# The first product of the first expert, first batch: from float32r halves to float16 pairs

## The chip, the core and the metric

The kernel runs on one core of a Trainium2 chip. The metric is the device time of one execution in microseconds, the median of several runs. A core has a matrix engine (TensorE, PE in the profile, with its weight loads as PEld), a vector engine (VectorE, DVE), an activation engine (ScalarE, ACT), GpSimd (POOL), and a queue engine (SyncE, SP) that issues the transfers. Every engine works through its own queue in the order in which the program was written, and waits by semaphores for the others.

## The reference

Attention over 2 batches, 8 heads, 576 positions and 64 channels, with rotary positions; its output, 1152 tokens of 512 numbers, goes through two experts in a row:

```python
def _moe_ref(x, w_a, w_b, w_out):      # 512 -> 1536 -> 512
    a = x @ w_a
    b = x @ w_b
    return (a * b @ w_out).astype(np.float32)

def _moe2_ref(x, w_in, w_out):         # 512 -> 2048 -> 512
    h = x @ w_in
    sp = np.where(h > 20.0, h, np.log1p(np.exp(np.minimum(h, 20.0))))
    g = h * np.tanh(sp)
    return (g @ w_out).astype(np.float32)
```

Inputs and output are float32. The weights arrive as float64 words (`in_w_dram`), and three VectorE instructions turn a block of 128 x 512 of them into float32 (`xw<-wr`).

## The kernel before

A number is kept as a high and a low part, and a product of two such numbers as three matrix products (high with high, high with low, low with high: `PASSES`). The parts are either both float16 after scaling by a power of two, or float32r, a rounded float32 that the matrix engine takes in one pass.

A recording layer (`Plan`) collects every operation with a priority (`at(t)`), a planned cost and its dependences, and then writes out one fixed order for every engine (`Plan.order`). `any_` operations go to VectorE or GpSimd, as the planner sees fit. So constants such as `W_LEAD`, `U0`, `U1` or `G` change no arithmetic; they change priorities, and by them the order.

The stages in order of time, with "unit" for one block of 128 query rows of a head (72 units in all):

- Attention of batch 0 (units 0 to 35, `attend0`), whose end overlaps the next.
- Attention of batch 1 (units 36 to 71, `attend`): scores `s`, row maximum `m` on VectorE, exponential on ScalarE, split `pp` into float16 pairs, a transposing DMA `pt`, product with the values `o`, and a transpose `xt` into `x`, again split into two parts. Woven into it, as matrix work that is always ready, lie layer 1 of the first expert for batch 0 (`layer1(0)`: for each of 12 steps f the tiles of w_a and of w_b, k = 0 and 1, each for 256 and for 320 tokens, 12 matrix instructions per tile) and then layer 2 (`layer2(0)`).
- Layer 1 and layer 2 for batch 1 (`layer1(1)`, `layer2(1)`), with 27 blocks of the second expert's weights converted ahead (`store_ahead`).
- The second expert, in two token groups (`hidden_two`, `accumulate`).

In `layer1(0)` a weight block is converted, copied to float32r high (ACT `w<-xw`), its remainder taken by `any_`, kept in DRAM as float32 (`ka<-xw`), and its absolute sum taken on ScalarE (`junk`, into `w_sum`). After layer 1 one matrix instruction adds `w_sum` over the partitions (`w1s`), and `power` turns the sums into powers of two, up and down (`w_up`, `w_dn`). `layer1(1)` loads the float32 blocks back (`wc<-ka`) and splits them with these scales into float16 pairs (ACT and DVE `w<-wc,w_up`); there the tokens of batch 1 are float16 pairs too. So batch 0 multiplies float32r and batch 1 float16, in the same shapes.

Of the kernel before, what the change touches and what calls it, by code (L numbers as in the profile page):

```python
# [38 lines left out]
FSLACK = 1300  # L39
FBIAS = 200  # L40
MARGIN = 0
D1 = 6
D4 = 2
# [357 lines left out]
W_LEAD = 7  # L401
PE_LAG = 0
LOAD_LEAD = 12
OFF = dict(S=-7, M=-8, E=-8, P=0.5, T=-0.5, V=4, N=-2, X=-4)
R0, R1 = 0.233, 0.73
U0, U1 = 1.766, 3.358
C0 = 8
F0 = 2
T_L1 = 3
Y_LATE = 30  # L410
Q_REST = 7
T_B = 12
LOAD_A = 16
HOLD = 40
# [10 lines left out]
YS = 12  # L425
S0_AT = 20
W3S = 28
# [4 lines left out]
O_LEAD = 2  # L432
FA = 1
# [12 lines left out]
VP = (8, 5, 8)  # L446
V_AT = 5
V_BOUND = 23
# [13 lines left out]
G = 1.495  # L462
# [17 lines left out]
def lo32(ap):  # L480
    return ap.bitcast(F32)
# [3 lines left out]
def kernel(ctx: ExitStack, tc: tile.TileContext, qk, v5, w1, w2, w34, tab, out):  # L485
# [43 lines left out]
    rings = dict(raw=(w_p, 3), xw=(w_p, 3))  # L529
# [13 lines left out]
    n_o = len(AHEAD) - NF2  # L543
# [7 lines left out]
    l1_dn = w_p.tile([128, 2 * NF1], F32, tag="l1_dn", name="l1_dn")  # L551
# [16 lines left out]
    def weights(  # L568
# [42 lines left out]
        if not split:  # L611
            return None
# [93 lines left out]
    x_dn = w_p.tile([128, 1], F32, tag="x_dn", name="x_dn")  # L706
# [222 lines left out]
    def transpose_x(p, part):  # L929

        early = p == SPLIT
        if not part:
            if p < NP:
                xT[p] = x_p.tile([128, 2, S], F32R, tag=f"x{p}", name=f"x{p}")
            else:
                xT[p] = x_p.tile([128, 2, 2 * S + 128], F16, tag=f"x{p}", name=f"x{p}")[:, :, 0:S]
# [18 lines left out]
        for t, c, n in parts:  # L955
            if p // NP in PLAIN1:
                act.copy(lo32(x[:, 0, c]), t[:, 0:n])
                continue
# [11 lines left out]
    def l1_tile(b, f, k, hf, w, t1):  # L970
# [3 lines left out]
        t = l_ps.tile([128, 512], F32, tag="l", name=f"l1_{b}_{f}_{hf}_{k}")  # L974
        i = 0
        for c in range(NM):
            x = xT[b * NP + c]
            if b in PLAIN1:
                pe.matmul(t[:, :n], lhsT=lo32(w[:, 0, c, :]), rhs=lo32(x[:, 0, sl]), start=(c == 0), stop=(c == NM - 1))
                continue  # L980
            for ws, xs in PASSES:
                pe.matmul(t[:, :n], lhsT=w[:, ws, c, :], rhs=x[:, xs, sl], start=(i == 0), stop=(i == 11))
                i += 1
        at(t1 - W_LEAD)
        if k == 0:
            ap, bufs = (rc_p, ASB) if b else (w_p, AS0)
            a_sb[hf] = ap.tile([128, S - TA], F32, tag="a_sb", name="a_sb", bufs=bufs)[:, :n]
            if b:
                act.activation(a_sb[hf], t[:, :n], AF.Copy, scale=l1_dn[:, 2 * f : 2 * f + 1])
            else:  # L990
                act.copy(a_sb[hf], t[:, :n])
        else:
# [7 lines left out]
            if b:  # L1000
                q = t[:, :n]
                dve.scalar_tensor_tensor(q, q, l1_dn[:, 2 * f + 1 : 2 * f + 2], p, op0=ALU.mult, op1=ALU.mult)
            else:
                q = p
                dve.tensor_tensor(q, p, t[:, :n], op=ALU.mult)
            act.copy(ab[:, 0, :], q)
            AB_ENG = dve if b else any_
            AB_ENG.tensor_tensor(ab[:, 1, :], q, lo32(ab[:, 0, :]), op=ALU.subtract)

    def layer1(b, t0, dt, early, between=None):  # L1010
# [3 lines left out]
        held = {}  # L1014
        for f, k, halves in steps:
            w = held.get((f, k))
            if w is None:
                if between:
                    between(2 * f + k, t0)
                i = 2 * f + k  # L1020
                w = weights(
                    t0 - W_LEAD,
                    w1[i],
                    hold=t0 - HOLD,
                    plain=b in PLAIN1,
                    cached=f"a{i}",
                    keep=f"a{i}" if i in KEEP1 else None,
                    stat=None if b else i,
                    half=w_up[:, i : i + 1] if b else None,
                )  # L1030
                w = held[f, k] = w.rearrange("p s (c j) -> p s c j", c=NM)
            for hf in halves:
                l1_tile(b, f, k, hf, w, t0)
                t0 += 2 * dt * (HALF[hf].stop - HALF[hf].start) / S
        return t0
# [146 lines left out]
    ab_cm = ab_p = l_cm = l_ps = None  # L1182
    plan.slack = SLACK[0]
    for n in range(NU):
# [8 lines left out]
        (attend0 if n < NU // 2 else attend)(n)  # L1193
        if n in PRE:
# [6 lines left out]
        if n == V_AT:  # L1201
# [3 lines left out]
            v_scale(1, NP)  # L1205
            v_split(1)
            v_split(2)
        if n == V_BOUND:
# [5 lines left out]
            dve.tensor_reduce(x_dn, v_mx[:, NP:], axis=AX.X, op=ALU.max)  # L1214
            dve.tensor_scalar_mul(v_x[:, NP:], v_up[:, NP:], x_dn)
# [23 lines left out]
    t = l_ps.tile([128, 512], F32, tag="l", name="w1s")  # L1239
    n1 = 2 * NF1  # L1240
    power(t[:, 0:n1], w_sum[:, 0:n1], w_up[:, 0:n1], w_dn[:, 0:n1])
    dve.tensor_scalar_mul(l1_dn, w_dn[:, 0:n1], x_dn)
# [9 lines left out]
    rings.update(raw=(rc_p, R6), xw=(rc_p, X6), rawc=(c_p, RC))  # L1252
# [167 lines left out]
    rings.update(raw=(w_p, 3), xw=(w_p, 3))  # L1420
# [142 lines left out]
```

## Time and profile before

| what | value |
|---|---|
| median of 3 runs | 562.15 us (561.83 to 562.51) |
| the profiled execution | 561.03 us, of which the span of the trace is 559.2 us |
| PE busy | 543.6 us, 97% of the span |
| PEld busy (weight loads, beside PE) | 429.3 us, 77% |
| DVE busy | 473.9 us, 85% |
| ACT busy | 356.1 us, 64% |
| POOL busy | 137.9 us, 25% |
| TensorE clock granted, mean over the span | 0.993 of full speed |

The ends of matrix instructions are modelled in the trace, and consecutive ones overlap. So the time that one costs is the distance from its start to the next start, not its duration. The bounds of the stages, read from the first and last instruction of their tiles: attention of batch 0 up to 94.2 us, attention of batch 1 with the last row maximum at 237.7, layer 1 of batch 1 from 263.5 to 337, layer 2 of batch 1 until the second expert begins at 372.

### The profile page before, as it was taken

The numbers are of one execution on the slowest core, as the hardware profiler recorded it, in microseconds if no ns is written. First come the engines' busy times: TensorE is split into PE (matmuls) and PEld (weight loads), VectorE is DVE, ScalarE is ACT, GpSimd is POOL, SyncE is SP. The second block draws the span as 40 slices with busy tenths as digits, with TensorE's granted clock in tenths as the row PEclk, the third lists the DMA queues.
The fourth block names the chain that finished last, engine by engine and source line by source line (L and its number), as shares of the span: only waits on it lengthen the run. The fifth ranks groups of instructions, "written<-read, shape, count | busy, mean of one in ns | idle before, by whom it ended". The sixth has DMA issues, their size and how long they took to land.

```text
span 559.2 us, 11791 instructions
## 1 busy us (share of the span) xinstructions
PE 543.6 (97%) x4416; PEld 429.3 (77%) x4416; DVE 473.9 (85%) x897; ACT 356.1 (64%) x731; POOL 137.9 (25%) x176
## 2 busy tenths in 40 slices
PE   7999999999999999999999999999999999999997
PEld 5778778889888988899876789997666776555553
DVE  5998999999999999977998899879999997554542
ACT  3879788677687786545676765369676545343440
POOL 1577657520221010110004002636430200000000
PEclk9899999999999999999999999999999999999999
DMA  8336556899999999999987379684779465431002
GB/s 318 108 107 208 170 163 186 229 231 210 280 234 216 256 247 252 272 235 373 386 275 273 95 248 349 237 273 147 263 270 331 170 199 193 136 100 62 1 0 94
DMA packets 92200, 117.40 MB, mean 210 GB/s; under 512 B 52080, under 2 KB 58224, under 8 KB 92144
## 3 DMA queue, kind: packets, MB, share of 16 engines
q1 hardware_dynamic: 92144, 116.66, 69.7%
q8 instruction: 34, 0.56, 0.4%
q14 instruction: 22, 0.18, 0.1%
HBM read 77.82 MB, written 27.53 MB: 188 GB/s over the span
## 4 chain that ended last, share of the span: by engine, by line
PE 77%; DVE 11%; ACT 4%; DMA 3%; issue 3%; SPq 1%; POOL 1%; DVEq 0%; ACTq 0%; POOLq 0%
PE l L397 31%; PE acc L397 16%; PE h L397 13%; PE s L397 7%; PE o L397 6%; PE tm L397 2%; DVE xw L397 2%; DVE m L397 2%; DMA wr<-in_w_dram 2%; DVE pp L397 1%; DVE w L397 1%; DMA qkr_k<-in_qk_dram 1%; DMA wc<-ka 1%; DVE wv L397 1%; SPq L397 1%
## 5 line engine op out<-in xcount | busy, mean ns | idle before, releaser
L397 PE MATMUL l<-x,w 128*128 128x320 f32 (+3 forms) x1152 | 157.8, 294 | 0.0
L397 PE MATMUL acc<-w,g 128*128 128x512 f16 (+1 forms) x432 | 103.4, 383 | 0.0
L397 DVE SCALAR_TENSOR_TENSOR xw<-wr,xw 128x512 uint32<-128x512 uint32 x136 | 96.9, 718 | 1.0
L397 PEld LDWEIGHTS <-wv 128*128 128x128 f16 x672 | 64.9, 98 | 27.7 <-issue 5.2
L397 PE MATMUL l<-ab,w 128*128 128x320 f32 (+1 forms) x576 | 81.3, 299 | 0.1
L397 PEld LDWEIGHTS l<-x,w 128*128 128x128 f32 x576 | 78.2, 190 | 3.0 <-issue 2.7
L397 PEld LDWEIGHTS l<-ab,w 128*128 128x128 f32 x576 | 77.5, 190 | 1.2 <-issue 0.8
L397 PEld LDWEIGHTS <-w 128*128 128x128 f16 x576 | 56.1, 98 | 14.4 <-issue 0.2
L397 PEld LDWEIGHTS <-g 128*128 128x128 f16 x372 | 36.3, 98 | 36.4
L397 DVE TENSOR_TENSOR hb<-h,hb 128x256 f32<-128x256 f32 (+1 forms) x112 | 47.7, 450 | 13.5 <-PE h L397 11.5
L397 PE MATMUL h<-sp,wv 128*128 128x256 f16 (+1 forms) x384 | 57.5, 286 | 0.5 <-DVE hb L397 0.5
L397 DVE TENSOR_REDUCE m<-s 128x1 f32<-128x576 f32 x72 | 51.9, 748 | 4.4 <-PE s L397 3.6
L397 PE MATMUL s<-qk 64*128 64x288 f32 x256 | 44.4, 439 | 2.3 <-DVE qk L397 1.4
L397 ACT ACTIVATE junk<-xw 128x512 f32<-128x512 f32 x51 | 32.5, 637 | 21.9 <-DVE xw L397 21.0
L397 ACT ACTIVATE hb<-hb,two_dn 128x512 f32<-128x512 f32 (+1 forms) x32 | 24.7, 773 | 32.2 <-DVE hb L397 32.2
L397 PE MATMUL h<-y,wv 128*128 128x256 f16 (+1 forms) x288 | 43.3, 286 | 0.4 <-DVE hb L397 0.3
L397 PEld LDWEIGHTS s<-qk 64*128 64x128 f32 x256 | 25.4, 190 | 10.9 <-issue 4.8
L397 ACT ACTIVATE s<-s,m 128x576 f32<-128x576 f32 x36 | 25.3, 715 | 11.6 <-DVE m L397 11.2
L397 DVE TENSOR_SCALAR xw<-wr 128x512 uint32<-128x512 uint32 x68 | 31.4, 471 | 0.2 <-DMA wr<-in_w_dram 0.2
L397 DVE SCALAR_TENSOR_TENSOR g<-hb,g_up,g 128x640 f16<-128x640 f32 (+1 forms) x27 | 24.1, 894 | 6.4 <-ACT g L397 5.7
L397 DVE SCALAR_TENSOR_TENSOR w<-wc,o_up,w 128x512 f16<-128x512 f32 x16 | 11.9, 750 | 20.3 <-ACT w L397 20.2
L397 POOL TENSOR_TENSOR w<-xw,w 128x512 fp32r<-128x512 f32 x10 | 13.7, 1365 | 62.3 <-ACT w L397 59.2
(186 smaller groups left out, 936.7 us busy)
## 6 DMA issues: line engine op xcount, KB each, us to landing
wr<-in_w_dram SPq DMA_DIRECT2D x68, 512.0 KB, 5.2
kc<-xw SPq DMA_DIRECT2D x32, 256.0 KB, 4.2
qkr<-in_qk_dram SPq DMA_DIRECT2D x14, 576.0 KB, 4.5
wc<-kc SPq DMA_DIRECT2D x27, 256.0 KB, 3.7
ka<-xw SPq DMA_DIRECT2D x24, 256.0 KB, 2.7
wc<-ka SPq DMA_DIRECT2D x24, 256.0 KB, 5.2
wt<-kc SPq DMA_DIRECT2D x16, 256.0 KB, 3.7
kwt<-wv SPq DMA_DIRECT2D x8, 512.0 KB, 3.8
```

The lines of the kernel that those rows point to most:

```text
L397: getattr(engine, method)(*map(real, args), **{k: real(v) for k, v in kw.items()})
```

## The change

Layer 1 of batch 0 multiplies float16 pairs too. For this the weights' scale has to be known before their step, not after the layer: `layer1(0)` loads the blocks of step f + 1 during step f (`load_w1`), adds their `w_sum` over the partitions with a matrix instruction into two spare columns of the bank of step f's own tile (`sum_w1`, after k = 0 and 320 tokens), makes the powers of two with four small VectorE instructions (`scale_w1`), and splits (`split_w1`). The tokens of batch 0 are scaled on their way out of `xt`. The pairs, not the float32 blocks, are kept in DRAM, and `layer1(1)` loads them straight into the weight tiles, with no split. The product of both scales now sits in the copy of the a-half (`ab_dn`), so the multiplication with the b-half has no scale any more. One block fewer is converted ahead (`AHEAD`: 26), so that one more step of the second expert's output product for the first token group runs in float32r. The order's constants are changed as well.

```diff
-U0, U1 = 1.766, 3.358
+U0, U1 = 1.654, 3.432
-F0 = 2
+F0 = 1
-QC = 128
+QC = 256
-AHEAD = (0, 2, 3, 5, 7, 8, 10, 12, 13, 15, 17, 18, 20, 22, 23, 25, 24, 26, 27, 28, 29, 30, 31, 32, 33, 34, 35)
+AHEAD = (0, 2, 3, 5, 7, 8, 10, 12, 14, 15, 17, 20, 22, 23, 24, 25, 26, 27, 28, 29, 30, 31, 32, 33, 34, 35)
-YS = 12
+YS = 9
-G = 1.495
+G = 1.373
...
-            act.copy(x[:, 0, c], t[:, 0:n])
-            hi = lo32(x[:, 0, c]) if p < NP else x[:, 0, c]
-            dve.tensor_tensor(x[:, 1, c], t[:, 0:n], hi, op=ALU.subtract)
+            if p < NP:
+                act.activation(hi, t[:, 0:n], AF.Copy, scale=x_up)
+                dve.scalar_tensor_tensor(lo, t[:, 0:n], x_up, hi, op0=ALU.mult, op1=ALU.subtract)
...
+        if g and SUM_LAST:
+            sum_w1(sums, g, g + 1)
...
-            if b:
-                act.activation(a_sb[hf], t[:, :n], AF.Copy, scale=l1_dn[:, 2 * f : 2 * f + 1])
-            else:
-                act.copy(a_sb[hf], t[:, :n])
+            act.activation(a_sb[hf], t[:, :n], AF.Copy, scale=ab_dn[:, b, f : f + 1])
...
+    def sum_w1(t, f0, f1):
+        pe.matmul(t, lhsT=ones_w, rhs=w_sum[:, 2 * f0 : 2 * f1], start=True, stop=True)
+
+    def scale_w1(t, f0, f1, t0):
+        c = slice(2 * f0, 2 * f1)
+        at(t0 - W_LEAD - P_LEAD)
+        up = w_up[:, c]
+        dve.tensor_scalar(up, t, 1e-30, 1e30, op0=ALU.max, op1=ALU.min)
+        up = up.bitcast(U32)
+        dve.tensor_scalar(up, up, 0x7F800000, 0x7F800000, op0=ALU.bitwise_and, op1=ALU.bitwise_xor)
+        dve.reciprocal(w_dn[:, c], up.bitcast(F32))
+        two = w_dn[:, c].rearrange("p (f t) -> p f t", t=2)
+        dve.scalar_tensor_tensor(
+            ab_dn[:, 0, f0:f1], two[:, :, 0], x_dn2[:, 0:1], two[:, :, 1], op0=ALU.mult, op1=ALU.mult
+        )
+
+    def split_w1(f, t0, dt):
+        for i in (2 * f, 2 * f + 1):
+            at(t0 - W_LEAD + i % 2 * dt)
+            w, up, r = new(0, i), w_up[:, i : i + 1], raw0[i]
+            act.activation(w[:, 0, :], r, AF.Copy, scale=up)
...
+                dve.scalar_tensor_tensor(w[:, 1, :], r, up, w[:, 0, :], op0=ALU.mult, op1=ALU.subtract)
+            held0[i] = w
+            kept[f"a{i}"] = d_p.tile([128, 2, 512], F16, tag=f"ka{i}", name=f"ka{i}")
+            sp.dma_start(kept[f"a{i}"], w)
```

What the new order does is shown at three places. The first is VectorE in layer 1 of batch 0, at step 6 (`l_0_6_...`: batch 0, step 6, token half, k). Before, the weights' remainder `w<-xw` stands wherever VectorE has room:

```order
L397 TENSOR_TENSOR w_2633<-xw_2527,w_2633 128x512
L397 RECIPROCAL den_1_1_2664<-den_1_1_2664 128x2
L397 TENSOR_TENSOR pp_2657<-s_2553,pp_2657 128x576
L397 TENSOR_TENSOR a_sb<-a_sb,l_0_6_0_1_2631 128x256
L397 SCALAR_TENSOR_TENSOR xw_2623<-wr_2490,xw_2623 128x512
L397 TENSOR_TENSOR w_2690<-xw_2533,w_2690 128x512
L397 TENSOR_REDUCE m_2708<-s_2687 128x1
```

After, at the same step, `w_0_14` is the first weight block of step 7:

```order
L397 TENSOR_SCALAR w_up<-l_0_6_1_0_2569 128x2
L397 SCALAR_TENSOR_TENSOR vhl_113<-v_1963,v_up,vhl_113 128x10x64
L397 TENSOR_SCALAR w_up<-w_up 128x2
L397 SCALAR_TENSOR_TENSOR xw_2589<-wr_2399,xw_2589 128x512
L397 RECIPROCAL w_dn<-w_up 128x2
L397 TENSOR_TENSOR a_sb<-l_0_6_0_1_2647,a_sb 128x256
L397 SCALAR_TENSOR_TENSOR ab_dn<-w_dn,x_dn_679 128x1
L397 SCALAR_TENSOR_TENSOR w_0_14_2670<-xw_2320,w_up,w_0_14_2670 128x512
```

Between the product of step 6 and the weights of step 7 there now lie eight VectorE instructions, the first of which reads a bank that the matrix engine has just written. On the matrix engine the same place, after, with step 6's two k tiles on either side of the new sum:

```order
L397 LDWEIGHTS w_0_12_2537
L397 MATMUL l_0_6_1_0_2569<-x_1655,w_0_12_2537 128x320
L397 MATMUL l_0_6_1_0_2569<-w_sum,ones_w 128x2
L397 LDWEIGHTS w_0_13_2575
L397 MATMUL l_0_6_0_1_2647<-x_820,w_0_13_2575 128x256
```

What follows there are 24 products of step 6 and 14 products of the attention, then step 7. The sums of steps 1 to 11 stand like this; step 0 has a sum of its own in the attention of batch 0.

The third place is VectorE at the end of the attention. `x<-xt` is the split of the last token block, `y_mx` the maxima of layer 2's eight tiles. Before, three of the eight come behind it (the third, `l_0_3_1`, seven instructions below these), with splits of batch 1's weights between them:

```order
L397 TENSOR_TENSOR x_4137<-xt_3968,x_4137 128x576
L397 TENSOR_REDUCE y_mx<-l_0_2_1_4073 128x1
L397 SCALAR_TENSOR_TENSOR w_4195<-wc_4156,w_up,w_4195 128x512
L397 SCALAR_TENSOR_TENSOR w_4207<-wc_4162,w_up,w_4207 128x512
L397 SCALAR_TENSOR_TENSOR w_4221<-wc_4167,w_up,w_4221 128x512
L397 TENSOR_SCALAR xw_4246<-wr_4172 128x512
L397 TENSOR_REDUCE y_mx<-l_0_3_0_4176 128x1
```

After, one does:

```order
L397 TENSOR_TENSOR pp_4152<-s_4072,pp_4152 128x576
L397 RECIPROCAL den_0_2_4182<-den_0_2_4182 128x2
L397 TENSOR_REDUCE y_mx<-l_0_3_0_4154 128x1
L397 RECIPROCAL den_1_3_4266<-den_1_3_4266 128x2
L397 TENSOR_TENSOR x_4283<-xt_4161,x_4283 128x576
L397 TENSOR_REDUCE y_mx<-l_0_3_1_4240 128x1
```

So the end of the attention has moved back against layer 2 of batch 0: on the matrix engine 90 products of that layer follow the last transpose `xt` before the change, and 21 after it.

## Rows read from the trace of the kernel before

**Rows 1.** Three stretches: length, busy us of PE, PEld, DVE, ACT, POOL; clock, DMA, GB/s:

```profile
94.20:237.70 143.50, 142.04 (x1331) 127.68 (x1329) 138.31 (x257) 106.28 (x250) 30.05 (x30) 1.00 1.01 243
237.70:263.50 25.80, 25.80 (x234) 25.17 (x232) 18.10 (x34) 12.04 (x26) 1.43 (x1) 1.00 1.02 295
263.50:337.00 73.50, 72.14 (x588) 57.30 (x587) 68.72 (x133) 50.77 (x113) 7.76 (x9) 1.00 0.76 263
```

**Rows 2.** PE in order of time at the end of the attention:

```profile
243.43 0.48 PE L397 MATMUL o<-vhl,pt 128*128 128x65 f16 x10
...
251.18 12.48 PE L397 MATMUL l<-ab,w 128*128 128x320 f32 x90
...
263.50 2.71 PE L397 MATMUL l<-x,w 128*128 128x256 f16 x21
```

**Rows 3.** PE in order of time, 295 to 305, with idle time in brackets:

```profile
299.19 1.05 PE L397 MATMUL l<-x,w 128*128 128x256 f16 x8
301.60 0.38 PE L397 MATMUL ys<-y_row,ones_w 1*128 1x1 f32 x2 [1.36 <-DVE y_row L397]
```

**Rows 4.** DVE groups from 263.5 to 337, the split of batch 1's weights:

```profile
L397 DVE SCALAR_TENSOR_TENSOR w<-wc,w_up,w 128x512 f16<-128x512 f32 x19 | 14.1, 743 | 0.4 <-ACT w L397 0.4
```

**Rows 5.** PE busy with tile l alone, in a float16 and a float32r stretch:

```profile
303.00:335.00 32.00, 32.00 (x264) 1.00 0.56 177
...
347.00:371.00 24.00, 22.92 (x176) 1.00 0.70 255
```

**Rows 6.** PE in order of time, 344 to 348: start us, us, instructions:

```profile
343.71 2.36 PE L397 MATMUL l<-ab,w 128*128 128x320 f32 x15
345.91 0.29 PE L397 MATMUL w3s<-w_sum,ones_w 128*128 128x16 f32 x2
346.05 2.16 PE L397 MATMUL l<-ab,w 128*128 128x256 f32 x16
```

**Rows 7.** The float32r stretch by shape: busy us, mean ns | idle before:

```profile
L397 PE MATMUL l<-ab,w 128*128 128x256 f32 x103 | 12.8, 283 | 0.0
L397 PE MATMUL l<-ab,w 128*128 128x320 f32 x73 | 11.3, 310 | 0.0
```

**Rows 8.** Weight loads of layer 1, whole span, same columns:

```profile
L397 PEld LDWEIGHTS l<-x,w 128*128 128x128 f32 x576 | 78.2, 190 | 3.0 <-issue 2.7
...
L397 PEld LDWEIGHTS <-w 128*128 128x128 f16 x576 | 56.1, 98 | 14.4 <-issue 0.2
```

**Rows 9.** DVE groups from 94.2 to 237.7: busy us, mean ns | idle before:

```profile
L397 DVE SCALAR_TENSOR_TENSOR xw<-wr,xw 128x512 uint32<-128x512 uint32 x56 | 39.2, 700 | 0.2
...
L397 DVE TENSOR_TENSOR w<-xw,w 128x512 fp32r<-128x512 f32 x21 | 16.3, 774 | 0.0
L397 DVE TENSOR_SCALAR xw<-wr 128x512 uint32<-128x512 uint32 x28 | 13.5, 490 | 0.2 <-DMA wr<-in_w_dram 0.2
L397 DVE TENSOR_TENSOR ab<-a_sb,ab 128x320 fp32r<-128x320 f32 x11 | 6.3, 570 | 0.0
...
L397 DVE TENSOR_TENSOR qkr<-qkr,cq 128x576 f32<-128x576 f32 x3 | 2.2, 749 | 0.0
```

**Rows 10.** The sum w1s on PE, then VectorE's reading of it in order of time:

```profile
L397 PE MATMUL w1s<-w_sum,ones_w x2: 265/267/269, 211.1 to 211.2; 128*128 128x24 f32 x2
...
214.32 0.17 DVE L397 TENSOR_SCALAR w_up<-w1s 128x24 f32<-128x24 f32 x1
214.41 0.68 DVE L397 SCALAR_TENSOR_TENSOR xw<-wr,xw 128x512 uint32<-128x512 uint32 x1
```

**Rows 11.** The chain that ended last, the last scores of the attention:

```profile
235.78 1.32 PE s L397 x8
```

**Rows 12.** Two pieces of the chain that ended last: start us, us, instructions:

```profile
422.02 2.59 PE acc L397 x12
...
444.35 1.16 PE acc L397 x5
```

**Rows 13.** One stretch of the second expert, columns as in the first group:

```profile
440.00:460.00 20.00, 20.00 (x123) 14.54 (x122) 19.69 (x40) 9.05 (x15) 0.00 (x0) 1.00 0.59 194
```

More of the change, by code (lines that the diff above doesn't have):

```diff
@@ L38 @@
 SLACK = (400, 0, 0, 0)
-FSLACK = 1300
-FBIAS = 200
+FSLACK = 1600
+FBIAS = 0
 MARGIN = 0
 D1 = 6
-D4 = 2
+D4 = 0
 LOOK = dict(pe=50, act=0, dve=0, pool=0, sp=0)
@@ L424 @@
 LAG4 = 4
-YS = 12
-S0_AT = 20
-W3S = 28
+YS = 9
+S0_AT = 16
+W3S = 26
 HBB = 2
@@ L432 @@
 O_LEAD = 2
+S_LEAD = 8
+P_LEAD = 6
+W1_AT = 28
+WG = ()
+SUM_LAST = 1
+W1N = 1
+XWB = 6
 FA = 1
@@ L445 @@
 WARM = 32
-VP = (8, 5, 8)
+VP = (8, 3, 10)
 V_AT = 5
-V_BOUND = 23
+V_BOUND = 22
 HAM = 3300
@@ L550 @@
     y_dn = w_p.tile([128, 2], F32, tag="y_dn", name="y_dn")
-    l1_dn = w_p.tile([128, 2 * NF1], F32, tag="l1_dn", name="l1_dn")
+    ab_dn = w_p.tile([128, 2, NF1], F32, tag="ab_dn", name="ab_dn")
     def power(t, m, up, dn):
@@ L705, with x_scale @@
     v_e = a_p.tile([128, B * NP], F32, tag="v_e", name="v_e")
-    x_dn = w_p.tile([128, 1], F32, tag="x_dn", name="x_dn")
+    x_dn = w_p.tile([128, 2], F32, tag="x_dn", name="x_dn")
+    x_dn2 = w_p.tile([128, 2], F32, tag="x_dn2", name="x_dn2")
+    x_up = w_p.tile([128, 1], F32, tag="x_up", name="x_up")
+    def x_scale(b):
+        d = x_dn[:, b : b + 1]
+        dve.tensor_reduce(d, v_mx[:, NP * b : NP * b + NP], axis=AX.X, op=ALU.max)
+        dve.tensor_tensor(x_dn2[:, b : b + 1], d, d, op=ALU.mult)
     def v_max(p):
@@ L974, in l1_tile @@
         t = l_ps.tile([128, 512], F32, tag="l", name=f"l1_{b}_{f}_{hf}_{k}")
+        sums = t[:, 480 : 482]
+        if g and not SUM_LAST:
+            sum_w1(sums, g, g + 1)
         i = 0
@@ L983, in l1_tile @@
                 i += 1
+        if g and SUM_LAST:
+            sum_w1(sums, g, g + 1)
         at(t1 - W_LEAD)
@@ L1013, in layer1 @@
         steps += [(f, k, (0, 1)) for f in range(early, NF1) for k in range(2)]
-        held = {}
+        held = {} if b else held0
         for f, k, halves in steps:
[L1016 to L1031, printed above, removed]
-            for hf in halves:
-                l1_tile(b, f, k, hf, w, t0)
+            if between:
+                between(2 * f + k, t0)
+            i = 2 * f + k
+            if b and i not in held:
+                at(t0 - W_LEAD)
+                w = held[i] = new(b, i)
+                plan.release = 1000 * (t0 - HOLD)
+                sp.dma_start(w, kept[f"a{i}"])
+                plan.release = 0
+            w = held[i].rearrange("p s (c j) -> p s c j", c=NM)
+            for hf in halves:
+                g = f + W1N if not b and not k and hf and f + W1N < NF1 else None
+                t1 = t0 + 4 * dt * W1N
+                if g:
+                    load_w1(g, t1)
+                t = l1_tile(b, f, k, hf, w, t0, g)
+                if g:
+                    scale_w1(t, g, g + 1, t1)
+                    split_w1(g, t1, dt)
                 t0 += 2 * dt * (HALF[hf].stop - HALF[hf].start) / S
@@ L1182 @@
     ab_cm = ab_p = l_cm = l_ps = None
+    first = T1 - D1 + T_L1
     plan.slack = SLACK[0]
@@ L1193 @@
         (attend0 if n < NU // 2 else attend)(n)
+        if n == W1_AT:
+            t = o_ps.tile([128, 512], F32, tag="o", name="w1s")[:, 0 : 2 * W1N]
+            for f in range(W1N):
+                load_w1(f, first + 2 * f)
+            at(first - W_LEAD - P_LEAD)
+            sum_w1(t, 0, W1N)
+            scale_w1(t, 0, W1N, first)
+            for f in range(W1N):
+                split_w1(f, first + 2 * f, 1.47)
         if n in PRE:
@@ L1238 @@
     at(T - 4)
[L1239 to L1242, printed above, removed]
+    w_two = w_dn[:, 0 : 2 * NF1].rearrange("p (f t) -> p f t", t=2)
+    dve.scalar_tensor_tensor(ab_dn[:, 1], w_two[:, :, 0], x_dn2[:, 1:2], w_two[:, :, 1], op0=ALU.mult, op1=ALU.mult)
     y0 = layer2(0, T, DT * G)
```

67 lines of the change are left out of this document (36 added, 31 removed).

## The prediction

> **What bounds the kernel now.** I read the stages first (busy time in stretches), then the distances between matrix instructions, then the vector engine's groups in the stage that changes, and the waits last. The page puts 97% on PE, but an average hides that two engines are full at once where this change works. In the attention of batch 1 PE is busy 142.0 of 143.5 us and DVE 138.3, which leaves DVE 5.2 us of idle time [rows 1]. From the last row maximum to layer 1 of batch 1 PE is still full and DVE is busy 18.1 of 25.8 us [rows 1]: there layer 2 of batch 0 runs alone, 90 products in one piece [rows 2]. In layer 1 of batch 1 PE loses 1.4 us, and one wait accounts for it: the matrix engine stands 1.36 us before the second `ys` product, until DVE has the maximum of one row [rows 3]. So matrix work saved counts only as far as DVE can follow in the attention, and DVE work saved in layer 1 of batch 1 (24 splits of 743 ns, 17.8 us [rows 4]) buys nothing but the end of that one wait, since PE runs there without a gap.
>
> **Float16 instead of float32r, 576 products.** In float16 264 products take 32.00 us [rows 5], as many of 256 as of 320 columns: 121.2 ns each. In float32r 15 products of 320 columns go from 343.71 to 345.91, 146.7 ns each [rows 6]; the 73 of these in the second stretch leave 12.2 of its 22.92 us for 103 products of 256 columns, 118.6 ns each [rows 5, 7]. In equal parts that is 132.7 ns. The difference, 11.5 ns, times 576 is 6.6 us less on PE.
>
> The weight load itself falls from 190 to 98 ns [rows 8], far more than 11.5, because loads lie beside products and beside each other. The Trainium skill's page "TensorE: Matmul & The Clock Gate" (section on weight-path modes) says that the fast weight load is off for float32 inputs; the trace agrees, with these 190 against 98 ns. The page "Perfetto Trace Analysis" (Identifying the Most-Contended Engine) judges the headroom of TensorE by the busy share of weight loads and not of products. By that rule the saving would be the difference of the two busy times [rows 8], 22.1 us; by the distances it is 6.6. That rule's time is a rival below.
>
> **The sums.** Each of 11 steps gets one float32 product with `ones_w`, two rows in the trace. Its like `w3s` takes 0.14 us until the next product starts, and the 16 products behind it, 2.16 us less the last one's 0.28 over 15 distances, stand 125 ns apart instead of 118.6, another 0.10 us [rows 6, 7]. That is 1.5 to 2.6 us; I take 2.0. PE's net is 4.6 us less (4.0 to 5.1).
>
> **What DVE gets in the attention.** Counted in the two orders between the first and the last row maximum of batch 1, in durations of [rows 9], [rows 4] and, for small instructions, the 0.09 us from one start to the next in [rows 10]:
> - 22 splits with a scale, 743 ns: +16.3 us; 16 plain remainders fewer, 774 ns: -12.4 us.
> - 44 small instructions for the scales: +4.0 us.
> - 4 remainders `ab` (570 ns) and 3 rotary products `qkr` (749 ns) go to GpSimd: -4.5 us. GpSimd is busy 30 of 143.5 us there [rows 1] and has the room.
> - conversions of layer 2's weights that stand earlier, 6 of 700 and 3 of 490 ns: +5.7 us. These were done behind the last maximum before, where DVE had time, so they aren't new work, but they delay the attention.
>
> The sum is +9.1 us. With its idle time of before, DVE reaches the last maximum 9.1 us later, at 246.8. Behind the last scores, which take 1.32 us [rows 11] and so start about 1.3 us before their last maximum, the new order has 89 products of layer 2 (132.7 ns, 11.8 us), 68 small ones of the values (at most 0.048 us each by [rows 2], 2 to 3.3 us) and a few transposes (0.5 us): about 15 us, where it had 26. Layer 1 of batch 1 then starts at 246.8 - 1.3 + 15 = 260.5 instead of 263.5 [rows 2]: 3.0 us earlier. If DVE's 5.2 us of idle time closed as well, PE's 4.6 us would be the bound. If DVE slips by a further 3 us, nothing is left. I take -3.0, nearer to DVE's row, because an engine at 96% has only hand-overs left as idle time.
>
> ScalarE's casts become scaled copies, somewhat longer, but it is busy 106 of 143.5 us [rows 1], and that cover holds. The transfers are as many and as large as before, in pieces half as long.
>
> **The `ys` wait.** With 24 splits gone from DVE, and 13 products instead of 8 between the two `ys` products in the new order, the 1.36 us [rows 3] should mostly go. From 0 to -1.4; I take -0.9, as PE needs the answer only 1.6 us (13 x 121 ns) after its question.
>
> **The tail.** Twelve products of 512 columns turn to float32r: 232 ns (1.16 us for 5) instead of 216 (2.59 for 12) [rows 12], +0.2 us. Their weight block is converted in the second expert instead of ahead: three conversions, 1.9 us by [rows 9], and a maximum, at most another 0.7, on a DVE that is 98% busy there [rows 13]. Hidden while PE keeps its lead; from 0 to +2.6, I take +0.3.
>
> **The start.** QC = 256 puts 576 more columns of rotary work before the first maximum. One instruction of 576 columns takes 749 ns [rows 9]: at most 0.7 us, given back later on DVE. I take +0.3.
>
> **Sum:** -3.0 - 0.9 + 0.2 + 0.3 + 0.3 = -3.1 us. Against the profiled execution (561.03 us) that is 557.9; that run lies 1.1 us under the median of 562.15, and the same step from the median gives **559.0 us**. A measurement of this kernel can tell about 0.2%, 1.1 us, from no change, so "faster" begins under 561.0.
>
> **Rivals.**
> 1. *All of the matrix time comes through.* DVE closes its idle time, layer 1 of batch 1 starts 4.6 to 5.1 us earlier, the `ys` wait goes whole: 556.0, at best 555. For it: DVE's work until that start falls by some 2 us in all, as 5.7 of the 9.1 only moved. Against it: 96% busy already. Chance 0.13.
> 2. *DVE swallows it.* The attention ends another 2 to 3 us later, as more GpSimd work (about 5.5 us) shares the memory with it; PE waits for the last tokens: 561 to 563. Chance 0.16.
> 3. *The scale loop stalls: slower.* Between a step's sum and the next step's first product PE has, in the middle of the 11 steps, 24 products (2.9 us) and 14 small ones (at most 0.7): 3.5 us. In that time DVE must do the eight instructions shown, 0.36 for four small ones, 0.70, 0.41, about 0.9 for the values' split and 0.74: 3.1 us, and ScalarE's high half lies between. Before, the reading of `w1s` came 3 us after the sum [rows 10]; nobody waited for it then. If every step is late by 0.3 us, the gain is gone; by 0.75 us, the time is 559.0 + 8 - 3 = 564, taking the 3 us of DVE's lag as run in the same shadow. Chance 0.17.
> 4. *Weight loads bound PE.* 22.1 us less gives 540. Against it: float32r products follow each other in 133 ns under loads of 190. Chance 0.01.
>
> **Numbers.** The forecast, a gain of 1.1 to 5 us, gets 0.53. Faster is forecast, first and fourth rival: 0.67; no change is the second, 0.16; slower the third, 0.17. For 8 in 10 the range runs from the first rival's end to the third's 564: 554.8 to 564.0. The forecast's own range is 557.2 to 561.0.
>
> **What the profile will show.** Right: distances of 121 ns in layer 1 of batch 0; the last row maximum at 245 to 248 us and layer 1 of batch 1 starting near 260; only some 20 products of layer 2 behind the last transpose; no wait of over 0.6 us at `ys`. The third rival shows as idle PE, or longer distances, between a sum and the next step's products, released by DVE or ACT `w`, eleven times. Wrong would be: the attention of batch 0 ending more than 1 us off 94.2, from the new constants, which I have at +0.3 only; or a new wait where batch 1's weights arrive straight from DRAM, with six tiles instead of an eight-deep ring ahead of the split. There each tile serves 24 products, 2.9 us, so six reach 14 us ahead of a transfer, and I cost it at nothing; if it fails, each late tile costs PE what it is late.

## The result, and the profile after

The change makes the kernel slower: 566.27 us (median of 6 runs, 564.89 to 568.99) against 562.33 us (6 runs). The ratio is 1.0072, with a 95% interval from 1.0050 to 1.0095. Forecast were 559.0 us and a range that ended at 564.0. The profiled execution of the changed kernel has a span of 563.1 us, that of before 559.2.

Busy time of the changed kernel in three stretches, which are cut at the same events as [rows 1] (first and last row maximum of batch 1, first product of layer 1 of batch 1, end of that layer); columns as there:

```profile
93.80:253.40 159.60, 149.11 (x1426) 117.76 (x1423) 151.06 (x309) 114.46 (x257) 35.27 (x35) 1.00 0.96 232
253.40:268.80 15.40, 15.18 (x156) 14.49 (x153) 5.24 (x12) 7.12 (x17) 0.66 (x1) 1.00 0.83 193
268.80:340.30 71.50, 71.50 (x584) 56.72 (x582) 63.05 (x129) 42.09 (x102) 7.59 (x9) 1.00 1.00 368
```

Set against [rows 1] this is the whole ledger. The attention begins 0.4 us earlier. It takes 159.6 instead of 143.5 us, so its last maximum comes at 253.4 instead of 237.7. What stands behind it shrinks from 25.8 to 15.4 us, and layer 1 of batch 1 starts at 268.8 instead of 263.5: 5.3 us later. That layer then takes 71.5 instead of 73.5 us, and the rest loses 0.6: 5.3 - 2.0 + 0.6 = 3.9 us, the difference of the two spans. In the attention DVE is busy 12.75 us longer than before and idle 8.5 instead of 5.2 us; PE, which was idle for 1.5 us, is now idle for 10.5.

VectorE's groups of the changed kernel in that attention (busy us, mean ns | idle before), which answer to [rows 9]:

```profile
L397 DVE SCALAR_TENSOR_TENSOR xw<-wr,xw 128x512 uint32<-128x512 uint32 x63 | 47.6, 763 | 0.1
L397 DVE SCALAR_TENSOR_TENSOR w<-xw,w_up,w 128x512 f16<-128x512 f32 x22 | 17.6, 802 | 0.0
L397 DVE TENSOR_SCALAR xw<-wr 128x512 uint32<-128x512 uint32 x31 | 15.4, 513 | 0.9 <-DMA wr<-in_w_dram 0.8
L397 DVE TENSOR_TENSOR w<-xw,w 128x512 fp32r<-128x512 f32 x5 | 3.4, 686 | 0.3 <-ACT w L397 0.3
L397 DVE TENSOR_SCALAR w_up<-l 128x2 f32<-128x2 f32 x11 | 1.7, 156 | 1.8 <-ACT a_sb L397 1.4 <-PE l L397 0.3
```

The counts are those of the prediction (22 splits, 16 plain remainders fewer, 11 rounds of small operations), with 7 and 3 conversions more instead of 6 and 3. The means are not: a conversion takes 763 instead of 700 ns, a split 802 instead of the 743 of [rows 4]. By their durations these longer instructions are 63 x 0.063 + 31 x 0.023 + 22 x 0.059 = 6.0 us; ends that overlap the next start are in that figure, so not all of it is added busy time.

TensorE's waits in the same attention (us in total, times, longest) were one line before:

```profile
PE s L397 <- DVE pp L397: 1.3, 3, 0.5
```

In the changed kernel they are these and two smaller ones:

```profile
PE l L397 <- ACT w L397: 2.1, 1, 2.1
PE s L397 <- DVE pp L397: 1.9, 2, 1.1
PE l L397 <- DVE w L397: 1.6, 5, 0.5
PE o L397 <- DMA pt<-pp: 1.5, 2, 0.9
PE s L397 <- DVE x L397: 1.0, 1, 1.0
PE l L397 <- ACT a_sb L397: 0.8, 1, 0.8
```

They are short and of many kinds. The longest stands between the first step's sum and the second step's first product:

```profile
105.55 0.28 PE L397 MATMUL l<-w_sum,ones_w 128*128 128x2 f32 x2
...
108.66 0.66 PE L397 MATMUL l<-x,w 128*128 128x256 f16 x4 [2.11 <-ACT w L397]
```

### The profile page after: what moved, and what is told of

Same layout as the page of the kernel before. It is cut to its first block, busy times and chain, and to the rows that moved or that the text cites. A ratio compares the mean times of both kernels' runs of the same rounds, so it can differ in the third digit from the quotient of the medians.

```text
span 563.1 us, 11831 instructions
## 1 busy us (share of the span) xinstructions
PE 540.8 (96%) x4438; PEld 409.8 (73%) x4438; DVE 459.7 (82%) x919; ACT 345.6 (61%) x705; POOL 135.5 (24%) x180
## 4 chain that ended last, share of the span: by engine, by line
PE 73%; DVE 14%; ACT 7%; DMA 3%; issue 2%; SPq 0%; POOL 0%; DVEq 0%; ACTq 0%; POOLq 0%
PE l L397 30%; PE acc L397 16%; PE h L397 13%; PE s L397 6%; PE o L397 5%; DVE xw L397 4%; PE tm L397 2%; DVE m L397 2%; DVE w L397 2%; DVE pp L397 1%; DMA pt<-pp 1%; ACT e L397 1%; ACT ptm L397 1%; DVE ab L397 1%; DMA qkr_q<-in_qk_dram 1%
## 5 line engine op out<-in xcount | busy, mean ns | idle before, releaser
L397 PE MATMUL l<-x,w 128*128 128x320 f16 (+1 forms) x1152 | 150.9, 286 | 5.4 <-ACT w L397 2.1
L397 PEld LDWEIGHTS <-w 128*128 128x128 f16 x1152 | 109.9, 99 | 37.2 <-issue 4.4
L397 DVE SCALAR_TENSOR_TENSOR xw<-wr,xw 128x512 uint32<-128x512 uint32 x136 | 99.0, 735 | 0.7
L397 PE MATMUL s<-qk 64*128 64x288 f32 x256 | 45.8, 439 | 3.7 <-DVE qk L397 1.5
L397 ACT ACTIVATE a_sb<-l,ab_dn 128x256 f32<-128x256 f32 (+1 forms) x48 | 24.0, 502 | 16.1 <-PE l L397 15.4
L397 DVE TENSOR_TENSOR pp<-s,pp 128x576 f16<-128x576 f32 x36 | 26.6, 751 | 3.6 <-ACT pp L397 3.6
L397 ACT CAST ptm<-tm 128x512 f16<-128x512 f32 x36 | 21.3, 592 | 11.8 <-PE tm L397 11.7
L397 DVE SCALAR_TENSOR_TENSOR g<-hb,g_up,g 128x640 f16<-128x640 f32 (+1 forms) x26 | 22.5, 870 | 7.1 <-ACT g L397 6.3
```

Of the source, the lines that this page charges most:

```text
L397: getattr(engine, method)(*map(real, args), **{k: real(v) for k, v in kw.items()})
```

## The experiments

Theory A: VectorE was as full as TensorE in the attention of batch 1, and its longer list is the loss. Rival B: the chain sum, scale, split, next step stalls TensorE. Rival C: the new numbers (priorities, order of weights, planner constants) cost, not the data path. Later a rival D: the places in the order hold TensorE, whatever VectorE has to do. Since the time of the kernel before differs a little from one group of runs to the next, each result is given as its ratio to before in the same group, with its 95% interval; the change stands at 1.0072. Differences from the change in us are between medians of different groups, in which before lay between 562.2 and 563.1.

### New plans: the numbers apart, and the chain loosened

One kernel has the new data path with the old numbers (`F0 = 1` stays), one the old path with the new numbers, one takes the scales two steps ahead, and one has fixed scales:

Old numbers, new path; of some twenty lines two stand for all:

```diff
-W_LEAD = 10
+W_LEAD = 7
...
-G = 1.373
+G = 1.495
```

> The changed data path (half-precision pairs, scales per step, pairs in DRAM) with the numbers of before in the tables and planner constants, except that the first expert's first step is still the only one done by halves. Against 566.3 changed and 562.3 before. Theory A (VectorE's work in the attention of batch 1 is what it lost): about as the change, 564 to 568, the last row maximum at 250 or later. Rival B (the scale chain of each step stalls TensorE): as the change as well, 565 to 570, since the chain is the same and its lead in the plan is 3 units shorter. Rival C (the new numbers put work where it collides, the data path is a gain): 558 to 562.

Measured: 572.33 us, 1.0176 (1.0140 to 1.0211).

New numbers, old path (the same lines the other way round, with `F0 = 1`).

> The kernel of before with the changed numbers alone (planner constants, order of the second expert's weights, where steps are placed); single-pass data path as before. Theory A: 561 to 564, since the numbers alone give VectorE almost no work more (one weight fewer converted ahead). Rival B: 561 to 563. Rival C: 565 or slower, with the attention of batch 1 longer by 5 us or more.

Measured: 572.96 us, 1.0189 (1.0157 to 1.0221).

Two steps ahead:

```diff
-W1N = 1
+W1N = 2
```

> The change with the scales taken two steps ahead (the weights of step f + 2 are summed in the bank of step f), so that the chain from the sum over four small VectorE operations to the split has a whole step more. VectorE's work is the same. Theory A: 565 to 568, VectorE's busy time between the first and the last row maximum of batch 1 at about 151 us as in the change, its end not earlier by more than 1 us. Rival B: 561 to 563, single TensorE waits for weights of over 1 us gone. Rival C: as the change, 565 to 567.

Measured: 573.07 us, 1.0203 (1.0161 to 1.0244).

Fixed scales:

```diff
-            sum_w1(t, 0, W1N)
-            scale_w1(t, 0, W1N, first)
+            pool.memset(w_up[:, 0 : 2 * NF1], 8.0)
+            pool.memset(w_dn[:, 0 : 2 * NF1], 0.125)
...
-            sum_w1(sums, g, g + 1)
...
-                    scale_w1(t, g, g + 1, t1)
```

> The change with fixed scales (8 for every weight of the first expert's first layers) in place of measured ones: it leaves out the eleven sums on TensorE and the 44 small VectorE operations inside the attention of batch 1; magnitudes are still taken, and the split, the pairs in DRAM and everything else stays. It takes about 7.5 us off VectorE and 2.5 us off TensorE in that attention. Theory A: last row maximum earlier by 6 to 9 us, layer 1 of batch 1 at 261 to 264, time 558 to 561. Rival B: gains what the chain's stalls cost and the sums, 2.5 to 5 us: 561 to 563.5. Rival C: under 3 us, 563.5 to 566.

Measured: 562.22 us, 0.9989 (0.9962 to 1.0016).

The first was missed by every theory. The second is what C said, but C falls with the first: the old numbers make the new path slower, not faster. The numbers of each kernel fit its own path, and with numbers made for the other the change is 6.1 us and before 10.6 us slower. How much VectorE does in the attention is not what decides there: with the old numbers and the new path it is busy for 6.6 us less than in the change, and the last maximum comes at 247.4 instead of 253.4, but the rest behind it takes 28.2 instead of 15.4 us and TensorE is idle for 16.8:

```profile
94.40:247.40 153.00, 136.25 (x1334) 104.53 (x1335) 144.47 (x295) 111.73 (x251) 27.36 (x27) 0.99 0.97 226
247.40:275.60 28.20, 28.08 (x250) 27.38 (x248) 24.03 (x46) 12.55 (x29) 0.00 (x0) 1.00 0.99 311
```

Its waits show what such a misfit looks like:

```profile
PE l L397 <- ACT w L397: 4.7, 4, 2.3
PE l L397 <- DVE w L397: 3.8, 4, 1.0
PE l L397 <- DVE a_sb L397: 3.2, 4, 1.2
PE o L397 <- DMA pt<-pp: 2.9, 3, 1.8
```

So the third says nothing of the chain: its plan is new as well. The fourth gains 4 us, which is B's figure and near A's, but its plan is new too. From here on, most experiments keep the order of one of the two kernels instruction by instruction and change only what is written out at the end of the planner, as here, where the low half of a first-layer weight becomes a memset:

```diff
                 engine, method, args, kw = op.call
...
+                if method == "scalar_tensor_tensor" and name.startswith("w1_0_"):
+                    engine.memset(real(out), 0.0)
+                    continue
                 getattr(engine, method)(*map(real, args), **{k: real(v) for k, v in kw.items()})
```

### The same order, one cost changed

No scale chain:

```diff
+    if method == "matmul" and name.startswith("l1_0") and "w_sum" in ins:
+        return True
+    if name in ("w_up", "w_dn") and 8 <= first < 96 and method in ("tensor_scalar", "reciprocal"):
...
+        return True
```

> Every instruction of the change in the order of the change, without the eleven sums of the first expert's weights during the attention of batch 1 and without the scale operations of steps 2 to 12 (one memset and one operation set them all to 8 once): it leaves out the measuring of those scales. Theory A (VectorE's work is the bound there; about 7 us of it go): 3 to 6 us below the change, 560 to 563. Rival B (the chain from sum to scale to split stalls TensorE, by most of the 8.5 us that TensorE waits more than before): 6 to 9 us below, 557 to 560. Since the order stays as it is, nothing here can come from a new plan.

Measured: 562.40 us, 0.9999 (0.9978 to 1.0020), 3.9 us under the change, in A's figure and not in B's. The attention takes 156.3 us with DVE busy 148.2:

```profile
96.50:252.80 156.30, 146.39 (x1404) 115.25 (x1401) 148.18 (x265) 113.60 (x257) 35.32 (x37) 1.00 0.94 237
```

Of the 3.3 us by which it is shorter than in the change, 2.9 are VectorE's busy time; its idle time is 8.1 us, with the chain it was 8.5. TensorE's longest wait stays too, since ScalarE keeps its order; so that wait is not the chain's arithmetic:

```profile
PE l L426 <- ACT w L426: 2.1, 1, 2.1
```

No low halves (the edit above):

> The change in its own order, but the low halves of the 24 first-layer weights of batch 1's attention are filled with zeros (a memset) instead of split off: it leaves out the low halves. About 24 x (802 - 150) ns = 15 us less on VectorE; the sums, the scales and the products are all there. Theory A: 7 us or more below the change, 559 or less. Rival B: 0 to 3 us below, 563 to 566.

Measured: 563.34 us, 1.0019 (0.9994 to 1.0044): about 3 us under the change, at the edge of B's figure and far from A's. A's figure counted on 15 us less work for VectorE; with the splits as memsets of 272 ns its busy time in the attention fell by 6.7 us, to 144.4. The attention shrank from 159.6 to 158.5 us only, and this speaks against A in its plain form. What the products waited for longest was ScalarE's high half, and that wait is untouched:

```profile
PE l L402 <- ACT w L402: 2.1, 1, 2.1
PE o L402 <- DMA pt<-pp: 2.1, 3, 1.0
```

More products:

```diff
+                    if SEEN[name] in (2, 3):
+                        getattr(engine, method)(*map(real, args), **{k: real(v) for k, v in kw.items()})
```

> The change in its own order, with two products of each of the 48 tiles of that layer taken twice (the sums are off by these): 96 products, about 96 x 122 ns = 11.7 us more on TensorE, nothing on any other engine. Theory A (TensorE has slack between VectorE's results): 3 to 7 us above the change, 569 to 573. Rival D (TensorE is still the bound and its waits are few and separate): 10 to 12 us above, 576 to 578.

Measured: 569.09 us, 1.0104 (1.0071 to 1.0137): 2.8 us above the change for 11.7 us of products (by the ratios 1.8). That is just below A's figure (3 to 7 us) and far from D's: TensorE no longer sets the time of this stage.

Half precision in the order of before:

```diff
-                xT[p] = x_p.tile([128, 2, S], F32R, tag=f"x{p}", name=f"x{p}")
+                xT[p] = x_p.tile([128, 2, 2 * S], F16, tag=f"x{p}", name=f"x{p}")[:, :, 0:S]
...
+            w = wp.tile([128, 2, 1024], F16, tag=tag, name=f"w{i}", bufs=bufs)[:, :, 0:512]
+            act.copy(w[:, 0, :], r)
+            any_.tensor_tensor(w[:, 1, :], r, w[:, 0, :], op=ALU.subtract)
```

> The kernel of before in its own order, with the activations and first-layer weights of that product held as half-precision pairs without any scale: it leaves out the scaling, so that small low halves are lost. 576 products take 11 ns less each, 6.6 us of TensorE; VectorE, ScalarE and GpSimd do the same operations as before. If TensorE bounds the attention of batch 1 in the kernel before: 5 to 6.6 us below before, 555.7 to 557.5. If VectorE is already the bound there (theory A in its strong form): 0 to 3 us below.

Measured: 559.77 us, 0.9944 (0.9923 to 0.9966): 3.3 us below before (1.9 to 4.3 by the interval), half of what the products save and between the two figures expected. The attention takes 142.3 us instead of 143.5, DVE busy 136.8 instead of 138.3, so the gain need not be the products' alone. Already in the kernel before, TensorE was not alone at the end of this stage.

GpSimd without its larger operations; this kernel leaves out seven rotations and fourteen low halves (`rows` counts row maxima):

```diff
+                if op.eng == "pool" and method == "tensor_tensor" and 36 <= rows < 72 and out.n >= 256:
+                    t = out.root.kw["name"]
+                    if t.startswith("qkr"):
+                        continue
+                    if t[0] == "w" or t.startswith("ab"):
+                        engine.memset(out.real().bitcast(U32), 0)
+                        continue
```

> The change in its own order, but GpSimd's larger operations with two operands in SBUF during the attention of batch 1 do no work beside VectorE: seven rotations of the next heads are left out, and fourteen low halves (of the layer-1 result and of second-layer weights) are filled with zeros instead of split off. VectorE's operations on two SBUF operands took 992 ns on average beside GpSimd and 684 ns alone, some 8 us in all. If that lengthening stalls TensorE: VectorE's busy time in that attention falls by 6 us or more and the time by 2 us or more, 564 or less. If it falls into slack: 565.5 to 567.

Measured: 561.53 us, 0.9972 (0.9947 to 0.9998): 4.7 us under the change, and VectorE's instructions, whose work is the same, are short again:

```profile
93.20:249.20 156.00, 148.25 (x1425) 117.36 (x1422) 144.01 (x308) 114.05 (x257) 14.66 (x28) 0.99 0.94 237
```

```profile
L410 DVE SCALAR_TENSOR_TENSOR xw<-wr,xw 128x512 uint32<-128x512 uint32 x63 | 44.1, 707 | 0.1
L410 DVE SCALAR_TENSOR_TENSOR w<-xw,w_up,w 128x512 f16<-128x512 f32 x22 | 16.2, 741 | 0.0
L410 DVE TENSOR_SCALAR xw<-wr 128x512 uint32<-128x512 uint32 x31 | 12.6, 421 | 1.1 <-DMA wr<-in_w_dram 1.1
```

### No chain, replanned

The chain taken out of the code's structure too, with loads and splits where before has them and a constant in each instruction, once with the old numbers and once with the new:

```diff
+                act.activation(w[:, 0, :], r, AF.Copy, scale=8.0)
+                dve.scalar_tensor_tensor(w[:, 1, :], r, 8.0, w[:, 0, :], op0=ALU.mult, op1=ALU.subtract)
```

> The changed data path (half-precision pairs, pairs kept in DRAM) with one fixed scale of 8 for all first-layer weights of the first expert, so that no split waits for a sum: it leaves out the measuring of those scales (magnitudes are still taken). Loads and splits stand where the kernel before has them (two steps by halves first), and all numbers of the tables and of the planner are those of before. If the chain as an order (a step's weights can't be split before the step before has been multiplied and summed) is what costs: 555 to 560, TensorE's waits over 150 ns in the attention of batch 1 back to some 3 us. If VectorE's longer split, or the traffic of the pairs to DRAM, costs: 561 to 566. If only a fresh choice of numbers could fit the new path at all: 568 or slower, as with the old numbers and the chain.

Measured: 564.86 us, 1.0028 (0.9995 to 1.0061).

> The same kernel with the numbers of the change. The numbers have moved with the chain (weights loaded and split earlier, one step by halves): without it they should be no better than those of before, 558 to 566; if the numbers of the change are simply worse for this chip, 565 or slower.

Measured: 563.67 us, 1.0022 (0.9990 to 1.0053).

Neither is faster than before, though both save the products' 6.6 us and have no chain. The old numbers don't fit this path either: its waits hold single ones of 2.7 us for the transposing transfer and 1.5 us for `w`. These two settle less than the runs in a fixed order.

### VectorE's share by itself

The first operation on the words of each of 24 weights is written out twice, in the order of before and in that of the change; then all three reliefs stand in one kernel:

```diff
+                if method == "tensor_scalar" and name in TWICE:
+                    getattr(engine, method)(*map(real, args), **{k: real(v) for k, v in kw.items()})
```

> The kernel of before in its own order, with the first operation on the words of each of the 24 first-layer weights of batch 1's attention done twice (the result is the same): 24 operations of 414 ns on VectorE, 9.9 us more, nothing on any other engine. This is the prediction's step by itself: it let VectorE's sum grow by 9.1 us at no cost, as TensorE's sum alone set the start of layer 1 of batch 1. By that step: 0 to 2 us above before. If VectorE was already as full as TensorE there: 6 us or more above before, 568 or more.

Measured: 569.56 us, 1.0128 (1.0088 to 1.0167): 7.4 us more for 9.9 us. The expectation put the prediction's step too harshly: the step did move the last maximum by VectorE's sum, and won the time back behind it by a shorter rest, which an unchanged order doesn't have. The two stretches around the last maximum, 151.5 and 25.7 us long, show just that step at work:

```profile
94.30:245.80 151.50, 146.09 (x1332) 129.97 (x1332) 145.92 (x276) 106.56 (x250) 29.57 (x29) 0.99 0.95 229
245.80:271.50 25.70, 25.70 (x233) 25.07 (x232) 18.16 (x34) 12.10 (x25) 1.43 (x1) 1.00 1.07 304
```

DVE has 7.6 us more, the attention takes 8.0 us more, its idle time is 5.6 us (5.2 before), and what follows is as long as in [rows 1].

> The change in its own order, with the first operation on the words of each of the same 24 weights done twice: 24 operations of 419 ns, 10 us more on VectorE. If VectorE bounds the first part of that attention: 5 us or more above the change, 571 or more. If its work falls into slack: 566 to 568.

Measured: 574.79 us, 1.0220 (1.0184 to 1.0256), 8.5 us above the change.

> The change in its own order with the three reliefs at once: scales fixed after the first step (the sums and 44 small operations go), low halves of the 24 weights as zeros, GpSimd's rotations left out and its low halves as zeros. VectorE loses some 26 us in the attention of batch 1, TensorE 2.5. If VectorE with GpSimd is what TensorE waits for: all waits over 150 ns but a microsecond or two go, 555 to 558. If the order itself holds TensorE (waits on ScalarE, on the transposing DMA, on places in the queues): about 560, as each relief alone.

Measured: 558.82 us, 0.9929 (0.9902 to 0.9957), 7.5 us under the change and between the two figures expected. DVE is busy 133.4 of 151.2 us in the attention, and TensorE's waits shrink to a few, the longest still the one in ScalarE's order:

```profile
PE l L440 <- ACT w L440: 2.7, 2, 2.1
PE o L440 <- DMA pt<-pp: 1.4, 4, 0.6
PE l L440 <- DVE w L436: 0.7, 1, 0.7
```

So VectorE's busy time counts in both directions, as A says: more of it costs nearly its whole length, less of it gives back a part. Of B, the chain's stalls, the runs in a fixed order show little, since without the chain VectorE's idle time (8.1 instead of 8.5 us) and TensorE's (9.9 instead of 10.5) hardly fall. The 2.1 us for ScalarE's `w`, which no relief removes, fit D. How the loss divides between A and D is not shown.

### What a move to GpSimd is worth

Some of GpSimd's operations of that attention go to VectorE at the same places in the order, first in the change:

```diff
+                if op.eng == "pool" and method == "tensor_tensor" and 36 <= rows < 72 and out.n >= 256 and (name.startswith("ab") or "cq" in ins):
+                    engine = self.real["dve"]
```

> The change in its own order, with thirteen of GpSimd's operations in the attention of batch 1 (nine low halves of the layer-1 result, four rotations) done by VectorE at the same places. VectorE gets 9 x 0.45 + 4 x 0.75 = 7 us more work of its own; GpSimd loses 14 us. By the prediction's term (an operation moved to GpSimd takes its whole duration off VectorE), VectorE's sum grows by 7 us: 570 to 573. If VectorE's operations on two SBUF operands wait for GpSimd's, as their lengths say, most of it comes back: 565 to 568.

Measured: 567.34 us, 1.0087 (1.0054 to 1.0120), the change's ratio within the intervals. Of the changed kernel with thirteen operations put back, the attention and two groups:

```profile
93.80:254.70 160.90, 149.93 (x1427) 118.00 (x1424) 152.44 (x322) 115.14 (x257) 22.30 (x22) 0.99 0.91 230
```

```profile
L407 DVE SCALAR_TENSOR_TENSOR w<-xw,w_up,w 128x512 f16<-128x512 f32 x22 | 16.2, 740 | 0.0
L407 DVE TENSOR_SCALAR xw<-wr 128x512 uint32<-128x512 uint32 x31 | 12.5, 417 | 0.9 <-DMA wr<-in_w_dram 0.9
```

VectorE does 13 operations more, some 7 us by their means, and is busy 1.4 us longer.

The same in the order of before, for the low halves of weights (`name[0] == "w"`):

> The kernel of before in its own order with half-precision pairs without a scale (as in the earlier run, 559.8; it leaves out the scaling), and the seven low halves of weights that GpSimd split in the attention of batch 1 done by VectorE at the same places: 7 x 0.68 = 4.8 us more on VectorE, 9.7 us less on GpSimd. If GpSimd's operations hold VectorE for as long as they take off it: 558 to 561. If they take their work off it whole: 563 to 565.

Measured: 560.40 us, 0.9955 (0.9936 to 0.9974), against 0.9944 without the move: no difference, again.

## Why the prediction was wrong

**Products and sums: right.** Taken from each start to the next, a float16 product takes 109 ns (256 columns) and 136 ns (320), the medians in the trace of the change, against 120 and 147 before: 11 ns less, as forecast. The sums take 2.5 us to the next product's start, 0.5 of it one wait; 2.0 were forecast.

**The step that failed is VectorE's sum in the attention, "+9.1 us", with its idle time unchanged.** The idea behind it was right: the last maximum moves by what VectorE gets (the run with 24 operations more shows it). But VectorE got 12.75 us, and its idle time rose by 3.3: the last maximum came at 253.4, not 246.8. The rest behind it took 15.4 us where 13.7 were forecast (15 less 1.3), so layer 1 of batch 1 began at 268.8, not 260.5:

```profile
251.43 1.37 PE L397 MATMUL s<-qk 64*128 64x288 f32 x8
252.73 0.64 PE L397 MATMUL o<-vhl,pt 128*128 128x130 f16 x8
...
268.80 0.94 PE L397 MATMUL l<-x,w 128*128 128x256 f16 x7
```

Of those 1.7 us 0.6 are a slip in the sum: what stands behind the last scores begins when they end, 0.7 us before the last maximum, and the prediction let its 15 us begin at their start. The rest itself took 16.1 us instead of 15.

**The term that was mis-sized is the -4.5 us for operations that go to GpSimd.** This is VectorE's busy time, after less before, with each operation charged from its start to the next start, so that the parts add up (in the prediction they are durations, the small operations apart):

| part | forecast, us | measured, us |
|---|---|---|
| splits with a scale | +16.3 | +16.0 |
| plain remainders | -12.4 | -11.9 |
| small operations for the scales | +4.0 | +3.8 |
| `ab` and `qkr` that go to GpSimd | -4.5 | -4.8 |
| conversions (10 more, 9 forecast) | +5.7 | +8.4 |
| two maxima `y_mx` and one `ptm` | not counted | +1.4 |
| all others | not counted | -0.2 |
| sum | +9.1 | +12.75 |

The seven operations did leave VectorE; what the term left out is that others grew. "GpSimd has the room" was the wrong question, because VectorE's operations on two SBUF operands, and the `xw` conversion with one, can stand still while GpSimd works; those that read the matrix engine's results do not (`m` takes 747 ns before and 749 after). Each operation that lies beside one of GpSimd's, set against the median of its kind alone, gives 7.1 us of stretching before and 10.5 after; with the thirteen operations put back it is 5.8. So by this estimate about 3.4 of the 4.5 us came back, and the move was worth some 1 us. The rest of the miss in the sum is mostly the 1.4 us that were not counted.

Two pieces of the same place in VectorE's order, from the changed kernel:

```profile
100.12 1.26 DVE L397 SCALAR_TENSOR_TENSOR xw<-wr,xw 128x512 uint32<-128x512 uint32 x1
101.30 1.62 DVE L397 TENSOR_TENSOR ab<-a_sb,ab 128x256 fp32r<-128x256 f32 x1
```

and GpSimd beside it:

```profile
99.43 3.21 POOL L397 TENSOR_TENSOR qkr<-qkr,cq 128x576 f32<-128x576 f32 x2
```

and the same two instructions in the run without GpSimd's rotations:

```profile
99.71 0.68 DVE L410 SCALAR_TENSOR_TENSOR xw<-wr,xw 128x512 uint32<-128x512 uint32 x1
100.31 0.41 DVE L410 TENSOR_TENSOR ab<-a_sb,ab 128x256 fp32r<-128x256 f32 x1
```

1.26 against 0.68 and 1.62 against 0.41 us: 1.8 us lost to two rotations that VectorE does in 0.75 us each. `ab` ends at 102.92, 0.28 us after the second rotation. The Trainium skill's page "SBUF — State Buffer" (section "SBUF: two separate sides") says that one pair of ports is shared by the two engines as an exclusive lock for the whole instruction, among others between a VectorE operation with two SBUF inputs and a GpSimd operation that reads SBUF; these lengths agree. The Trainium skill's page "Perfetto Trace Analysis" (Optimizing Scalar/DVE Operations) says that moving operations between those two might not help; the two runs that moved them back agree. With 12.75 in place of 9.1 us and nothing else changed, the prediction's own further steps would have ended 3.7 us later, at 562.7; the idle time and the rest behind the last maximum make up most of what is left.

**The idle time** rose by 3.3 us. VectorE's longest waits in that attention are these, where before the longest was 0.7 us:

```profile
DVE pp L397 <- ACT pp L397: 2.0, 1, 2.0
DVE w_up L397 <- ACT a_sb L397: 1.4, 4, 0.7
DVE y_mx L397 <- ACT y L397: 1.3, 2, 0.7
```

Only the second, before the first of the small operations, belongs to the scale chain, and it is no explanation: without the chain, in the same order, the idle time is 8.1 instead of 8.5 us, and the first and third are as long. So most of the 3.3 us are places in the new order, and what set them is not shown. The third rival priced the chain as eleven equal delays with a time of 564. Instead TensorE waits 2.1 us behind one step, and that wait stays without the chain; the sums, the 44 operations and their stalls together are worth 3.9 us in the change's own order, by VectorE's busy time above all. Part of them was in the forecast (2.0 on TensorE, 4.0 on VectorE).

**The second rival named the cause**, GpSimd's work beside VectorE's, but let it swallow the gain only. Taking GpSimd's operations away was worth 4.7 us, the chain 3.9, and both with the low halves 7.5; the effects overlap and don't add up. The first rival's condition, VectorE closing its idle time, came out the other way round (and its "at best 555" does not follow from its terms: 562.15 - 5.1 - 1.4 is 555.65). The fourth is answered by the distances: the weight loads are busy for 19.5 us less (429.3 to 409.8), and a product is 11 ns shorter.

**The `ys` wait went**, as forecast: layer 1 of batch 1 has no idle time at all and takes 2.0 us less, against 0.9 forecast (the wait was 1.4; what the other 0.6 are is not shown); the transfers straight from DRAM made no new wait. The start (0.4 us earlier; 0.3 later forecast) and the tail (+0.6; +0.5 forecast) were right within their size.

**What stays open:** what set VectorE's longer waits, and why the low halves are worth so little. VectorE lost nearly 7 busy us in that run, as in the one without GpSimd's work, and the attention shrank by 1.1 instead of 3.6 us. That the products wait for ScalarE's high half in either case fits, but no run took ScalarE's part away in the same order. Nor is it shown how much better the change's numbers could be chosen; the misfits of 6.1 and 10.6 us say that a plan's numbers weigh more than the change itself.

**A version that beats both:** the kernel before in its own order with half-precision pairs, 559.77 us, 0.9944 of before. It has no scales; what that costs with weights much smaller than these, no run here shows.

## What to carry to other kernels

Where two engines are both over 95% busy in a stage, price every microsecond that a change puts on the second one before counting what it saves on the first: here 9.9 us on VectorE cost 7.4, and 6.6 us off TensorE brought 3.3. An operation moved from VectorE to GpSimd isn't off VectorE's list when both read SBUF: thirteen put back added 1.4 us there, not 7. And in a kernel with a planned order, tell a cost apart by changing the instruction in the order that stands, since a new plan can add microseconds of its own (6.1 and 10.6 here).

## What was not expected of the hardware

Beside GpSimd not only VectorE's operations on two SBUF operands grew, but also the `xw` conversion with a single one, `TENSOR_SCALAR` on 512 words: 419 ns alone, up to 1623 ns. Filling with zeros on GpSimd (`MEMSET`, 311 to 526 ns) left operations on two SBUF operands at their usual length, but not this conversion, which took 527 ns beside one in the run without GpSimd's larger operations and 578 and 655 in the run with all reliefs. A split by a per-partition scale takes 741 to 744 ns alone (medians); with the scale as a constant in the instruction (the two replanned runs without the chain) the same split takes 680, as long as the plain remainder.
